# The mark of group 1: batch 4's loads wait for the second of batch 3's five query transposes

## The chip, the cores and the metric

The kernel runs on one core of a Trainium2 chip. The metric is the device time of one execution in microseconds, as the median of several runs; lower is better. A core has five engines with a queue of instructions each: TensorE (PE, matrix products), VectorE (DVE), ScalarE (ACT), GpSimd (POOL) and SyncE (SP, which here only issues DMAs). They run side by side and wait for each other by semaphores. DMAs are issued by SP, ScalarE and GpSimd and are all carried out by the same 16 DMA engines.

## The reference

Eight batches of eight heads with 576 positions and 64 dimensions go through causal attention in a window of 128 positions with a distance bias, and the result, as 4608 tokens of 512 features, goes through a gated feed-forward block. In short:

```python
scores = scale * np.matmul(q, k.transpose(0, 1, 3, 2))
mask = (rel >= 0) & (rel < window)            # window = 128
scores = np.where(mask, scores + bias[None], -1000000000.0)
attn = softmax(scores)
x = np.matmul(attn, v)  ->  (4608, 512)
out = (gelu(x @ w_gate) * (x @ w_val)) @ w_out     # d_ff = 1536
```

## The kernel before

The feed-forward block works in nine groups `g` of 512 tokens: twelve products `gate_val` (L612) per group with the activation on ScalarE (L618) and the product on VectorE (L619), then sixteen pieces of the output product (L648), whose results ScalarE or VectorE copies to `osb` (L653) and SP stores (L638). Attention for later batches is laid between these by an order written out by hand. The loop over `g` calls, after the gate and value products, the list `steps(g)`. For `g` = 1 that list holds batch 2's scores and values, then batch 3's scores: `("s2", 3, 0)` and `("s2", 3, 2)`, two head pairs each (L288), with three pieces of the output product between them. For `g` = 2 it holds batch 3's values (L490, scaled into `xT` by L547) and batch 4's scores. The scores' order on TensorE begins with blocks of queries from position 384 on, so the last part of the transposed queries is needed early.

Inputs of a batch b go through two buffers each, chosen by b % 2. GpSimd loads `qs`, `ks` and `vb` with a cast to bfloat16 (`load`, L108, five DMAs each of at most 128 positions). SP then transposes them by DMA in `transposes_dma(b)`: all of `ks` at once into `kT` (L170), then `qs` in five parts of 128 positions into `qT` (L174):

```python
for j in range(5):
    nc.sync.dma_start_transpose(
        out=qT[b % 2][:, :, 128 * j:128 * j + 128], in_=qs[b % 2][:, j, :])
```

SP's queue is in order: at the head of `g` = 1 the six transposes of batch 3, then that group's stores, then at the head of `g` = 2 the six transposes of batch 4, which wait for batch 4's loads.

When GpSimd begins its loads is set by marks: a copy of two elements into the tile `mark`, which waits for the data it reads, with the loads behind it in GpSimd's queue. There is one at the end of `g` = 0 (L952, on batch 2's key transpose, ahead of the loads of q and k of batch 3), one at the head of `g` = 1 (L914, ahead of q and k of batch 4 and v of batch 3) and one in each group from 2 on, in the tenth gate product (L936).

The reciprocal sums of batch 3 are made in `g` = 2: `sums4` (L426), a gather by ScalarE's DMA queue into `rd` (L439), and a spread over the partitions into `rb` (L445), which L547 reads.

Of the kernel before, what the change touches and what calls it, by code (L numbers as in the profile page):

```python
# [30 lines left out]
def kernel(  # L31
# [10 lines left out]
    nc = tc.nc  # L42
# [27 lines left out]
    def keep_busy(ps, n, w=64):  # L70
        for _ in range(n):
# [18 lines left out]
    mark = consts.tile([1, 2], BF16, name="mark")  # L90
# [3 lines left out]
    qT, kT = ([consts.tile([128, 4, 640], BF16, name=f"{nm}T{i}") for i in range(2)]  # L94
              for nm in "qk")
# [16 lines left out]
    def load_qk(b):  # L112
        load(qs[b % 2], q, b)
        load(ks[b % 2], k, b)

    def load_v(b, js=range(5)):
        load(vb[b % 2], v, b, js, 64)
# [44 lines left out]
    def transpose(b, what, c, copy):  # L162
        ps = bank().bitcast(BF16)
        for n, lo in ((0, 0), (1, 384)):
            transpose_runs(b, n, what, c, ps[:, lo:576])
        for n, lo in ((0, 0), (1, 384)):
            untangle(copy, b, n, what, c, c + 1, ps[:, lo:576])

    def transposes_dma(b):
        nc.sync.dma_start_transpose(  # L170
            out=kT[b % 2].rearrange("p c (j t) -> p (c j) t", t=128),
            in_=ks[b % 2].rearrange("p j x -> p (j x)"))
# [3 lines that stand above are left out]
# [191 lines left out]
    def add(b, c0, copy=None, what=(0, 1)):  # L367
        hs = slice(2 * c0, 2 * c0 + 4)
        P = Ps[b % 2].rearrange("p h (n y) -> p h n y", y=64)[:, hs]
        to = T.rearrange("p h (n y) -> p h n y", y=64)[:, hs]  # L370
        if 0 in what:
            for x in (0, 1):
                half = slice(64 * x, 64 * x + 64)
                nc.vector.tensor_tensor(  # L374
                    out=to[half, :, x:x + 7:2], in0=P[half, :, 0:10:3], in1=P[half, :, 1:11:3],
                    op=ALU.add)
            nc.vector.tensor_copy(out=to[0:64, :, 8], in_=P[0:64, :, 12])
            nc.vector.tensor_tensor(
                out=to[64:128, :, 8], in0=P[64:128, :, 11], in1=P[64:128, :, 12], op=ALU.add)
        if 1 in what:  # L380
            for x in (0, 1):
                half, n = slice(64 * x, 64 * x + 64), 4 - x
                (copy or nc.vector.tensor_copy)(
                    out=to[half, :, x + 1:x + 2 * n:2], in_=P[half, :, 2:3 * n:3])
# [30 lines left out]
    def sums4(b):  # L415
        ps = bank()
        for s, at in ((0, 0), (1, shape(b, 0)[1])):
            first, w = shape(b, s)
            mms = []
            for h in range(H):  # L420
                for x in (0, 1):
                    t = first + w * x
                    g, a = 2 * x + h // 4, 32 * (h % 4)
                    mms.append((g, ones8[:, a:a + 32], T[:, h, t:t + w]))
            for n, (g, lhsT, rhs) in enumerate(in_turn(mms)):
                nc.tensor.matmul(  # L426
                    out=ps[32 * g:32 * g + 32, at:at + w], lhsT=lhsT, rhs=rhs,
                    start=n < 4 and s == 0, stop=True, skip_group_check=True)
        for s, at in ((0, 0), (1, shape(b, 0)[1])):
            first, w = shape(b, s)  # L430
            nc.vector.reciprocal(row(b)[:, first:first + w], ps[:, at:at + w])  # L431
# [3 lines left out]
    def gather(b):  # L435
        flat[b] = d_pool.tile([H, S], FP32, name="rd")
        for s in (0, 1):
            lo, w = shape(b, s)
            nc.scalar.dma_start(  # L439
                out=flat[b][:, lo:lo + 2 * w].rearrange("h (x t) -> x h t", x=2),  # L440
                in_=sumrow[b][0:128:8, lo:lo + w])

    def spread_dma(b):
        for i in (0, 1):
            nc.scalar.dma_start(  # L445
                out=recip[b][64 * i:64 * i + 64, :, :],
                in_=flat[b][i:H:2, :].unsqueeze(0).to_broadcast((64, 4, S)))
# [149 lines left out]
    def gate_val(g, f, lo=0, hi=512, later=None):  # L597
        if g not in hid:
            hid[g] = h_pool.tile([128, NF, 512], BF16, name="hT")
        t0 = 512 * g % RING  # L600
        n = hi - lo

        if n > 256 or lo >= 384:
            pg, pv = bank()[:, 0:n], bank()[:, 0:n]
            order = [(w, ps, c, c == 0) for w, ps in ((wg, pg), (wv, pv)) for c in range(4)]
        else:
            ps = bank()
            pg, pv = ps[:, 0:n], ps[:, n:2 * n]
            order = [(w, ps, c, w is wg and c == 0)
                     for cs in ((0, 1), (2, 3)) for w, ps in ((wg, pg), (wv, pv)) for c in cs]  # L610
        for w, ps, c, begins in order:
            nc.tensor.matmul(  # L612
                out=ps, lhsT=w[:, c, 128 * f:128 * (f + 1)], rhs=xT[:, c, t0 + lo:t0 + hi],
                start=begins, stop=(c == 3), skip_group_check=n <= 256 and lo < 384)

        def act():
            gl = g_pool.tile([128, 512], BF16, name="gelu")
            nc.scalar.activation(out=gl[:, 0:n], in_=pg, func=AF.Gelu)  # L618
            nc.vector.tensor_tensor(out=hid[g][:, f, lo:hi], in0=pv, in1=gl[:, 0:n],  # L619
                                    op=ALU.mult)  # L620

        if later is None:
            act()
        else:
            later.append(act)
# [10 lines left out]
    def store():  # L636
        for args in stores:
            nc.sync.dma_start(**args)  # L638
        stores.clear()
# [65 lines left out]
    for h in (0, 2, 4, 6):  # L705
        for w, src in ((0, q), (1, k)):
            (nc.scalar if w and h == 0 else nc.sync).dma_start(
                out=raw[w][h // 4].rearrange("p (h x) -> p h x", h=4)[:, h % 4:h % 4 + 2, :],
                in_=src[0][h:h + 2, 0:384, :].rearrange("h (p r) d -> p h (r d)", r=3))
# [42 lines left out]
    def masks_of_last_blocks(lo, hi):  # L752
        nc.vector.tensor_copy(out=emask[:, lo:hi, 192:384], in_=emask[:, lo:hi, 0:192])
        nc.vector.tensor_copy(out=emask[:, lo:hi, 384:512], in_=emask[:, lo:hi, 0:128])
        for x, at in ((0, 128), (1, 0)):
            half = slice(64 * x, 64 * x + 64)
            nc.vector.tensor_copy(out=emask[half, lo:hi, 512:576], in_=emask[half, lo:hi, at:at + 64])
# [63 lines left out]
    for step in zip(*(inverse_first(0, x, sums_a[x]) for x in (0, 1))):  # L821
        for do in step:
            do()
    dve(out=pairs1.rearrange("p x (h d) -> p h x d", d=64),
        in_=vb[1].rearrange("p j x -> p (j x)")[:, 0:1536].rearrange(
            "p (h x d) -> p h x d", h=H, x=3))
# [45 lines left out]
    for n in range(2):  # L872
        nc.gpsimd.dma_start(
            out=wo[:, 6 * n:6 * n + 6, :],
            in_=moe_w_out[768 * n:768 * n + 768, :].rearrange("(c p) f -> p c f", p=128))
# [33 lines left out]
    for g in range(NG):  # L909
        if 1 <= g < B - 2:  # L910
            transposes_dma(3 if g == 1 else g + 2)
        if g == 1:

            nc.gpsimd.tensor_copy(out=mark, in_=qT[1][0:1, 0, 512:514])  # L914
            load_qk(4)
            load_v(3)
        for f in range(9 if g == 0 else 0, NF):
            gate_val(g, f)
            if g == 2 and f == 2:
                add(3, 2, act, (1,))  # L920
            if g == 0 and f == 10:
                masks_of_last_blocks(0, 8)
            if g == 0 and f in (9, 11):
                for c in (0, 1) if f == 9 else (2, 3):
                    for w in (0, 1):
                        transpose(1, w, c, (act, dve)[w])
            if 2 <= g < B - 1:
                if f == (4 if g == 2 else 3):
                    sums4(g + 1)
                if f == (6 if g == 2 else 5):  # L930
                    gather(g + 1)
                if f == (8 if g == 2 else 7):
                    spread_dma(g + 1)
                if f == 9 and g + 2 < B:

                    nc.gpsimd.tensor_copy(out=mark, in_=hid[g][0:1, f, 0:2])  # L936
                    if g + 3 < B:
                        load_qk(g + 3)
                    load_v(g + 2)
        if g == 0:  # L940
            nc.gpsimd.memset(Ps[0][:, :, 0:64], 0.0)
            for t in (qs[1], ks[1]):
                nc.gpsimd.memset(t[64:128, 4, :], 0.0)
        for item in steps(g):
            if isinstance(item, int):
                out_part(g, item)
            else:
                RUN[item[0]](*item[1:])
        store()
        if g == 0:  # L950

            nc.gpsimd.tensor_copy(out=mark, in_=kT[0][0:1, 0, 512:514])  # L952
            load_qk(3)
            load_v(2)
# [30 lines left out]
```

## Time and profile before

| | |
|---|---|
| median of three runs | 342.26 us (342.24 to 343.99) |
| the profiled execution's own time | 342.35 us |
| its span, first to last instruction | 340.6 us |
| TensorE busy | 328.9 us, 97% of the span |
| VectorE, ScalarE, GpSimd busy | 192.4, 172.1, 106.4 us |
| mark L914 starts | 94.06 us |
| GpSimd's loads of q and k of batch 4, v of batch 3 | issued 94.59 to 107.36 us |
| SP's transposes of batch 3 | issued 79.57 to 91.06 us |
| SP's transposes of batch 4 | issued 108.06 to 120.12 us |

Times inside the profile count from the first instruction of the span. A line of a timeline gives start, length, engine, source line, operation, tiles, and in brackets the engine's idle time before it with what ended it. A line of the table of waits gives who waited for whom: total us, times, longest. A DMA's issue and its landing are different times; its semaphore climbs in sixteen steps, and a waiter is let go at the sixteenth.

### The profile page before, as it was taken

How to read it: one execution, taken by the hardware profiler on the slowest of the kernel's cores; microseconds unless marked ns; L12 is line 12 of the kernel's file. 1: busy time of each engine (PE TensorE's matmuls, PEld its weight loads, DVE VectorE, ACT ScalarE, POOL GpSimd, SP SyncE). 2: the span in 40 equal slices, each digit the busy share in tenths (PEclk: the TensorE clock that was granted, in tenths of full speed). 3: DMA queues.
4: the chain of work that ended last, by engine and by line, in shares of the span. 5: the costliest groups of instructions: out<-in, count | busy, mean ns of one | idle time of the engine just before them, and what ended most of it. 6: DMA issues, size and time to landing. Idle time of an engine off the chain costs nothing.

```text
span 340.6 us, 8147 instructions
## 1 busy us (share of the span) xinstructions
PE 328.9 (97%) x3299; PEld 169.9 (50%) x3342; DVE 192.4 (56%) x358; ACT 172.1 (51%) x321; POOL 106.4 (31%) x142
## 2 busy tenths in 40 slices
PE   7999999999999988999999999999999999999996
PEld 6677555444554444445544454445444544444443
DVE  7878666445679536944695469635974323303320
ACT  7974597438896328433753357244723133223322
POOL 5975763571095075007700680040000000000000
PEclk9999999999999999999999999999999999999999
DMA  8999999999599999959994999398106110020002
GB/s 211 170 195 192 204 165 142 148 190 170 108 167 151 128 172 189 208 126 162 187 181 85 160 182 190 70 164 108 64 3 140 64 62 1 2 93 31 0 33 92
DMA packets 150026, 43.49 MB, mean 128 GB/s; under 512 B 133572, under 2 KB 142948, under 8 KB 149988
## 3 DMA queue, kind: packets, MB, share of 16 engines
q0 software_dynamic: 107424, 18.10, 68.9%
q1 hardware_dynamic: 39104, 18.55, 23.3%
q10 hardware_dynamic: 3460, 6.32, 8.9%
q8 instruction: 26, 0.43, 0.5%
q14 instruction: 12, 0.10, 0.1%
HBM read 43.65 MB, written 9.53 MB: 156 GB/s over the span
## 4 chain that ended last, share of the span: by engine, by line
PE 79%; DMA 6%; ACT 5%; SPq 4%; issue 2%; POOL 2%; DVE 1%; POOLq 0%; DVEq 0%
PE ps L612 48%; PE ps L648 21%; DMA ks<-in_k_dram 3%; PE ps L490 3%; DMA qT<-qs 3%; ACT P L219 2%; PE ps L288 2%; SPq L174 2%; PE ps L668 2%; PE ps L206 1%; SPq L170 1%; POOL ks L108 1%; POOL qs L108 1%; PE ps L682 1%; PE ps L426 1%
## 5 line engine op out<-in xcount | busy, mean ns | idle before, releaser
L619 DVE TENSOR_TENSOR hT<-ps,gelu 128x512 bf16<-128x512 f32 (+3 forms) x119 | 74.0, 636 | 92.6 <-PE ps L612 84.9
L618 ACT ACTIVATE gelu<-ps 128x512 bf16<-128x512 f32 (+3 forms) x119 | 65.4, 558 | 101.0 <-PE ps L612 96.8
L612 PE MATMUL ps<-xT,wv 128*128 128x512 bf16 (+3 forms) x472 | 112.9, 359 | 0.4
L612 PE MATMUL ps<-xT,wg 128*128 128x512 bf16 (+3 forms) x461 | 111.7, 359 | 0.8
L648 PE MATMUL ps<-wo,hT 128*128 128x512 bf16 x375 | 87.8, 379 | 2.0 <-issue 1.3
L612 PEld LDWEIGHTS <-wv 128*128 128x128 bf16 x476 | 45.3, 98 | 48.5
L612 PEld LDWEIGHTS <-wg 128*128 128x128 bf16 x476 | 44.7, 98 | 48.0 <-issue 0.3
L648 PEld LDWEIGHTS <-hT 128*128 128x128 bf16 x396 | 37.0, 98 | 43.7
L219 ACT ACTIVATE P<-ps 128x512 bf16<-128x512 f32 (+1 forms) x108 | 51.2, 578 | 4.0 <-PE ps L288 2.7
L653 ACT COPY osb<-ps 128x512 f32<-128x512 f32 x28 | 16.4, 587 | 50.5 <-PE ps L648 50.3
L222 DVE TENSOR_TENSOR P<-P,emask 128x768 bf16<-128x768 bf16 x60 | 31.3, 556 | 18.9 <-ACT P L219 17.2
L108 POOL DMA_DIRECT2D vb<-in_v_dram x40 | 33.9, 878 | 8.3 <-DMA ks<-in_k_dram 4.9
L108 POOL DMA_DIRECT2D qs<-in_q_dram x30 | 25.2, 857 | 6.1 <-DMA wo<-in_moe_w_out_dram 4.3
L108 POOL DMA_DIRECT2D ks<-in_k_dram x30 | 25.4, 893 | 3.4 <-DMA qs<-in_q_dram 3.4
L936 POOL COPY mark<-hT 1x2 bf16<-1x2 bf16 x4 | 0.7, 174 | 73.1 <-DVE hT L619 73.1
L547 DVE TENSOR_TENSOR xT<-ps,rb 128x512 bf16<-128x512 f32 (+3 forms) x34 | 14.6, 500 | 7.9 <-PE ps L490 4.8
L490 PE MATMUL ps<-P,vb 64*64 64x192 bf16 (+2 forms) x752 | 16.8, 220 | 0.2
L490 PEld LDWEIGHTS <-vb 64*64 64x64 bf16 x752 | 14.2, 107 | 3.1 <-issue 2.6
L374 DVE TENSOR_TENSOR T<-P 64x1024 bf16<-64x1024 bf16 x20 | 13.7, 686 | 0.6
L288 PE MATMUL ps<-qT,kT 64*64 64x192 bf16 (+2 forms) x440 | 9.3, 224 | 2.2 <-DMA qT<-qs 1.2
L288 PEld LDWEIGHTS <-kT 64*64 64x64 bf16 x440 | 7.7, 107 | 6.8 <-issue 6.8
L431 DVE RECIPROCAL r<-ps 128x128 f32<-128x128 f32 (+1 forms) x10 | 9.8, 1021 | 0.0
(92 smaller groups left out, 184.8 us busy)
## 6 DMA issues: line engine op xcount, KB each, us to landing
out_dram<-osb SPq DMA_DIRECT2D x35, 256.0 KB
rb<-rd ACTq DMA_DIRECT2D x10, 576.0 KB
vb<-in_v_dram POOLq DMA_DIRECT2D x32, 128.0 KB, 6.6
qs<-in_q_dram POOLq DMA_DIRECT2D x24, 128.0 KB, 5.7
ks<-in_k_dram POOLq DMA_DIRECT2D x24, 128.0 KB, 6.1
wo<-in_moe_w_out_dram POOLq DMA_DIRECT2D x2, 768.0 KB, 14.8
wg<-in_moe_w_gate_dram POOLq DMA_DIRECT2D x5, 256.0 KB, 8.3
wv<-in_moe_w_val_dram POOLq DMA_DIRECT2D x5, 256.0 KB, 8.9
```

Source lines behind the costliest of these rows:

```text
L108: nc.gpsimd.dma_start(out=t[at:at + n, j, :].rearrange("p (h d) -> p h d", h=H), in_=src[b][:, 128 * j:128 * j + n, :].rearrange("h p d -> ...
L219: nc.scalar.activation(out=dst, in_=src, func=AF.Exp, scale=0.125)
L222: nc.vector.tensor_tensor(out=dst, in0=dst, in1=m, op=ALU.mult)
L288: mm = nc.tensor.matmul(out=ps[64 * x:64 * x + 64, col:col + w], lhsT=keys(b, c, m)[half, :], rhs=qT[b % 2][half, c, q0:q0 + w], start=Tru ...
L374: nc.vector.tensor_tensor(out=to[half, :, x:x + 7:2], in0=P[half, :, 0:10:3], in1=P[half, :, 1:11:3], op=ALU.add)
L490: mm = nc.tensor.matmul(out=out, lhsT=lhsT, rhs=prob(b)[half, c, i, col:col + q1 - q0], start=all(t[2] != u for t in todo[:n]), stop=True, ...
L547: nc.vector.tensor_tensor(out=xT[:, c, at:at + e - a], in0=src, in1=recip[b][:, c, a:e], op=ALU.mult)
L612: nc.tensor.matmul(out=ps, lhsT=w[:, c, 128 * f:128 * (f + 1)], rhs=xT[:, c, t0 + lo:t0 + hi], start=begins, stop=(c == 3), skip_group_che ...
L618: nc.scalar.activation(out=gl[:, 0:n], in_=pg, func=AF.Gelu)
L619: nc.vector.tensor_tensor(out=hid[g][:, f, lo:hi], in0=pv, in1=gl[:, 0:n], op=ALU.mult)
L648: nc.tensor.matmul(out=acc[g], lhsT=hid[g][:, f, 128 * t:128 * (t + 1)], rhs=wo[:, f, :], start=(f == 0), stop=(f == NF - 1))
L653: (nc.vector.tensor_copy if g < B - 2 and t in by_dve.get(g, (0,)) else nc.scalar.copy)(out=osb, in_=acc[g])
```

## The change

The mark L914 reads another part of `qT[1]`: columns 128 and 129, which the second of batch 3's five query transposes writes, instead of columns 512 and 513, which the fifth writes.

```diff
         if g == 1:
 
-            nc.gpsimd.tensor_copy(out=mark, in_=qT[1][0:1, 0, 512:514])
+            nc.gpsimd.tensor_copy(out=mark, in_=qT[1][0:1, 0, 128:130])
             load_qk(4)
             load_v(3)
```

The order of instructions on every engine is the same. The waits that the program derives from it differ in a few places: the mark's own; the loads of batch 4 and 5 that could lean on the mark's wait for a semaphore now name it themselves (the fifth part instead of the second); and when `qT[1]` is written again for batch 5, the second part's transpose, not the fifth's, waits for the mark.

## The prediction

> **What bounds the kernel now.** I read the page first. TensorE is busy 97% of the span and the clock row is 9 in every slice, so any time that TensorE stands still goes straight into the end, and only waits of TensorE matter. Then I read the table of waits between 85 and 131 us, the stretch in which batch 3's queries are transposed and batch 4's are loaded and transposed (engine and line <- what was waited for: us, times, longest):
>
> ```profile
> POOL mark L914 <- ACT osb L653: 15.5, 1, 15.5
> ...
> DVE xT L547 <- DMA rb<-rd: 3.1, 1, 3.1
> ...
> PE ps L288 <- DMA qT<-qs: 1.2, 1, 1.2
> ...
> PE ps L288 <- DVE xT L547: 0.9, 1, 0.9
> ```
>
> TensorE stands still twice for batch 4's scores (L288): 0.9 us for banks that VectorE had not emptied, because it waited 3.1 us for the spread reciprocals `rb`, and 1.2 us for the transposed queries `qT`. The chain that ended last (start, us, what) tells where `qT` was late:
>
> ```profile
> 93.34 0.57 ACT osb L653
> ...
> 93.94 0.04 POOLq L914
> ...
> 94.59 0.49 POOL qs L108
> ...
> 102.20 5.59 DMA ks<-in_k_dram
> ...
> 108.06 3.87 SPq L170
> ...
> 118.90 9.79 DMA qT<-qs
> 128.69 0.04 issue
> 128.73 0.81 PE ps L288 x27
> ```
>
> It runs from the mark (L914) through GpSimd's loads of batch 4, SP's transposes and the fifth query transpose into the scores at 128.73. So the edited wait lies on the path. The view gives ScalarE's copy (L653) as the mark's releaser; I do not believe it. The program's wait on ScalarE is for an old count, the 62nd (61st after the change), from the copies of batch 1's transposes near 42 us. The trace's record of semaphore steps, which no view prints, has the sixteenth step of the fifth query transpose at 93.91, where that copy also ends.
>
> TensorE's timeline shows what those waits cost, and a third place, batch 3's scores at 93.55:
>
> ```profile
> 93.55 1.25 PE L288 MATMUL ps<-qT,kT 64*64 64x64 bf16 x44
> ...
> 96.78 0.87 PE L288 MATMUL ps<-qT,kT 64*64 64x64 bf16 x44
> ...
> 127.18 0.40 PE L288 MATMUL ps<-qT,kT 64*64 64x64 bf16 x4 [0.90 <-DVE xT L547]
> 128.73 0.84 PE L288 MATMUL ps<-qT,kT 64*64 64x192 bf16 x40 [1.16 <-DMA qT<-qs]
> ```
>
> At 93.55 the same 44 matmuls take 1.25 instead of 0.87 us: they already use batch 3's fifth transpose the moment it lands (93.91). Anything that makes that landing later stops TensorE at once. The same work in the pass for batch 5, 161.51 to 164.85, has no wait:
>
> ```profile
> 123.75:129.57 5.82, 3.77 (x56) 1.98 (x56) 2.88 (x6) 1.01 (x2) 2.77 (x4) 1.00 1.67 171
> 161.51:164.85 3.34, 3.34 (x56) 1.79 (x56) 2.46 (x6) 0.77 (x2) 3.34 (x5) 1.00 2.02 190
> ```
>
> (stretch: its length, then busy us and instructions of PE, PEld, DVE, ACT, POOL, then clock, DMA share, GB/s.) Fifty-six TensorE instructions take 5.82 us for batch 4 and 3.34 for batch 5.
>
> **What the Trainium skill says.** "DMA: Bandwidth & Descriptors", section "Queues, rings and completion order": each of the 16 DMA engines takes turns between the queues that have work for it. So loads running beside a transpose take turns from it; the trace agrees (batch 2, below). The same page, "Why a DMA increments its semaphore by 16 and not by 1": all data has landed only at the sixteenth step, since each engine posts one. The trace agrees: fifteen steps of the fifth transpose are there by 92.30, the last at 93.91. The same page, "Latency and other measured facts", gives about 1 us to the first byte of a GpSimd DMA; here the first packet of batch 4's loads comes at 96.17, 1.58 us after the issue at 94.59, and I use that.
>
> **The change, part by part.** Nothing is added or removed: the mark is still one two-element copy of 0.17 us. What changes is when it passes, and with it fifteen DMA issues (five q, five k, five v).
>
> *When it passes.* The second query transpose lands (sixteenth step) at 88.98, the fifth at 93.91: 4.93 us earlier. The mark then starts at 94.06 - 4.93 = 89.13, the first load is issued at 89.66, its first packets come at 91.24. The loads' own further waits are for batch 2's transposes, which landed by 73.23. GpSimd was idle from 78.5, so nothing on it is displaced, and its next job after these loads is the mark L936 at 118.38.
>
> *The gain.* Before, the keys landed at 107.79 and SP began batch 4's transposes at 108.06. Now the same loads run 4.93 us earlier but beside more traffic: the fifth transpose (about 0.85 us of all engines) and two output stores of 256 KB (128 packets of 2048 B at 86 ns over 16 engines, 0.69 us each). At most 2.2 us are lost, so the keys land at 102.9 to 105.1. SP's one key and five query transposes follow: 3.9 us of issue and five times 1.3, to 113.6 to 115.8; with 1.25 us (alone) to 3.9 us (shared) to land, the last is there between 114.9 and 119.7. TensorE wants it at 126.3, so the 1.16 us wait goes. It had been long because the third to fifth transposes ran into the spread `rb` (issued 114.52 and 115.26) and batch 5's loads. Now they are out of `rb`'s way. In batch 5 `rb` took 149.63 to 157.95, 8.3 us; here that makes 114.5 + 8.3 = 122.8 instead of 125.73, before the products end (123.6), so the 0.90 goes too. Gain: 5.82 - 3.34 = 2.48 us. Bounds: 1.5 if `rb` stays as late, 2.9 if all of the difference between this pass (97.58 to 135.76, 38.18 us) and batch 5's (135.76 to 171.04, 35.28) goes.
>
> *The loss.* Transposes one to four have landed by 90.97, before the loads' packets begin. The fifth, issued 89.84 to 91.06, sends packets from 91.0 on, while the loads start at 91.24. The nearest case is batch 2, whose loads for batch 3 were issued at 63.84 while its third to fifth transposes were still to come:
>
> ```profile
> 61.66 6.59 SPq L174 DMA_TRANSPOSE qT<-qs  x5
> ...
> 63.84 4.21 POOL L108 DMA_DIRECT2D qs<-in_q_dram  x5
> ```
>
> (the first line is SP's timeline, the second GpSimd's.) From end of issue to sixteenth step, batch 2's five took 1.27, 1.25, 3.88, 3.89 and 4.98 us: the first two alone, the rest beside loads. Batch 3's took 1.26, 2.78, 1.24, 1.22 and 2.85, all without loads; the second and fifth met a 16 KB instruction fetch on one engine (1.19 us at 86.31, 1.00 us at 91.86). Fifth transpose after the change: 91.06 + 3.89 = 94.95 without the fetch, and up to 1.61 more (2.85 - 1.24) with it, 96.56. I take 95.2, near the low end, because it starts 0.24 us ahead of the loads where batch 2's third started level with them. So batch 3's scores slip by 95.2 - 93.91 = 1.3 us, with all that follows on TensorE, and none of it is caught up: the next wait of TensorE is the one that disappears. Bounds: 0 if it is through before the loads count, and 91.06 + 4.98 + 1.61 - 93.91 = 3.7. The slip also moves sums and `rb` 1.3 us later together with TensorE's need of them, so the gain stands.
>
> *Sum.* -2.48 + 1.3 = -1.2 us: span 339.4 from 340.6, execution 341.15 from 342.35. The median before (342.26) is 0.09 below that execution, so I predict 341.1. About 0.5%, 1.7 us, is what a measurement tells from no change: faster means under 340.55, slower over 343.97.
>
> **Rivals.**
> (a) The fifth transpose slips under 0.8 us, because most of its packets pass first. For: its packets need only 0.85 us, and the loads come thinly at first. Against: in batch 2 every transpose behind the start of loads lost 2.6 us. Time: 2.48 - 0.4 = 2.1 faster, 340.2.
> (b) The slip eats the gain, 2.5 to 3.7 us, if the fetch at 91.86 meets an engine whose share of the fifth transpose is unfinished. Time: 342.3 to 343.5.
> (c) Slower: the fifth transpose waits as batch 4's third did. That one, issued by 116.85, had its sixteenth step at 126.79, 9.9 us later. At that lag batch 3's scores start at 101.0, a slip of 7.1, net +4.6: 346.9. It decides from a lag of 5.3 us on (2.85 + 2.48), and shows as slower from 7.0 on. Against: there the engines were held by `rb`'s packets of 2304 B, up to 1.6 us each; the loads' 128 B packets take 32 ns.
> (d) Nothing moves, because the mark really waits for ScalarE's copy at 93.91, as the view says: 342.3. Against: the count it waits for.
>
> **Numbers.** The forecast, slip 0.8 to 2.5, has 0.50, its own range 340.6 to 342.3; (a) 0.25, (b) 0.10, (c) 0.10, (d) 0.05. Faster: (a) and a sliver of the forecast, 0.27. Slower: (c), and what of (b) coincides with the low gain of 1.5, 0.14. Same: 0.59. The range 339.8 to 343.5 takes in (a), the forecast, (b) and (d), and leaves out (c) and a full gain with no slip.
>
> **What would show it.** Right: the mark near 89.1 and the first load near 89.7; batch 3's first 44 matmuls of L288 ending near 96.1 instead of 94.8, with a wait on `qT` there; SP's key transpose of batch 4 between 103 and 105.4; no wait before batch 4's scores, the 56 instructions in 3.3 to 3.6 us. Wrong: the mark still at 94; a slip over 2.5 us; or a wait left before batch 4's scores, from `rb` or from `qT`.

## The result, and the profile after

The changed kernel takes 342.62 us (median of 22 runs), and the kernel before, run beside it, 342.62 as well. The ratio is 0.9984, with a 95% interval from 0.996 to 1.0009: -0.5 us, between -1.4 and +0.3. It compares means without the few executions of both kernels that ran slow as a whole, which is why it lies under 1 though the medians agree. The forecast was 341.1 us against 342.26, a ratio of 0.9966. The profiled execution of the changed kernel took 342.81 us and its span is 341.0 us. Single executions of either kernel lie between 339 and 347 us here, so one profile against another says nothing on the total; its parts can be compared.

The table of waits of the changed kernel, between 85 and 131 us (who waited for whom: total us, times, longest):

```profile
POOL mark L914 <- ACT rb L521: 10.5, 1, 10.5
...
DVE xT L547 <- DMA rb<-rd: 2.4, 1, 2.4
...
PE ps L288 <- DMA qT<-qs: 1.9, 1, 1.9
...
PE ps L288 <- DVE xT L547: 0.6, 2, 0.3
```

The mark's wait is 5 us shorter. The view again names a ScalarE instruction that happened to end then; the second query transpose had its sixteenth step at 89.67. TensorE still waits for `qT`, now 1.9 us instead of 1.2, but at another place, as its timeline shows (start, length, engine, line, tiles, and in brackets the idle time before):

```profile
93.58 0.28 PE L288 MATMUL ps<-qT,kT 64*64 64x64 bf16 x4
95.76 0.84 PE L288 MATMUL ps<-qT,kT 64*64 64x192 bf16 x40 [1.90 <-DMA qT<-qs]
...
98.58 0.87 PE L288 MATMUL ps<-qT,kT 64*64 64x64 bf16 x44
...
127.87 0.61 PE L288 MATMUL ps<-qT,kT 64*64 64x64 bf16 x16
128.78 0.27 PE L288 MATMUL ps<-qT,kT 64*64 64x192 bf16 x2 [0.29 <-DVE xT L547]
129.38 0.64 PE L288 MATMUL ps<-qT,kT 64*64 64x192 bf16 x26 [0.33 <-DVE xT L547]
```

The wait for `qT` is at batch 3's scores (95.76), on its fifth transpose. At batch 4's scores the wait for `qT` is gone, and two short ones on VectorE's scaling remain. GpSimd's and SP's timelines show the moved work:

```profile
89.81 0.17 POOL L914 COPY mark<-qT 1x2 bf16<-1x2 bf16 x1 [10.51 <-ACT rb L521]
90.34 4.20 POOL L108 DMA_DIRECT2D qs<-in_q_dram  x5 [0.35 <-issue]
```

```profile
106.21 3.71 SPq L170 DMA_TRANSPOSE kT<-ks  x1
109.98 6.93 SPq L174 DMA_TRANSPOSE qT<-qs  x5
```

The loads start 4.25 us earlier (90.34 for 94.59), the transposes of batch 4 only 1.85 (106.21 for 108.06). The chain of the changed kernel has turned accordingly. It enters batch 3's scores from the fifth transpose, and batch 4's from the spread `rb`:

```profile
90.48 5.24 DMA qT<-qs
95.72 0.04 issue
95.76 0.81 PE ps L288 x27
...
116.36 10.36 DMA rb<-rd
...
126.84 2.49 DVE xT L547 x4
129.34 0.04 issue
129.38 0.64 PE ps L288 x19
```

And the stretch of 56 TensorE instructions before and in batch 4's scores, 125.41 to 130.02 (length, busy us and instructions of PE, PEld, DVE, ACT, POOL, clock, DMA share, GB/s), is 4.61 us long where it was 5.82:

```profile
125.41:130.02 4.61, 3.99 (x56) 1.99 (x56) 2.88 (x6) 1.37 (x3) 4.23 (x6) 1.00 2.18 186
```

In this pair of profiles 1.21 us were gained at batch 4 and 1.77 lost at batch 3 (batch 3's first scores end at 96.57 for 94.80).

### The profile page after: what moved, and what is told of

Read it like the earlier page. It is cut to its first block, busy times and chain, and to the rows that moved or that the text cites. A ratio compares the mean times of both kernels' runs of the same rounds, so it can differ in the third digit from the quotient of the medians.

```text
span 341.0 us, 8148 instructions
## 1 busy us (share of the span) xinstructions
PE 329.0 (96%) x3299; PEld 169.9 (50%) x3342; DVE 192.5 (56%) x358; ACT 172.3 (51%) x321; POOL 106.4 (31%) x142
## 4 chain that ended last, share of the span: by engine, by line
PE 71%; DMA 16%; POOL 4%; SPq 3%; DVE 2%; issue 2%; ACT 0%; ACTq 0%; DVEq 0%; POOLq 0%
PE ps L612 44%; PE ps L648 20%; DMA ks<-in_k_dram 6%; DMA wo<-in_moe_w_out_dram 5%; DMA rb<-rd 3%; PE ps L490 3%; PE ps L288 2%; POOL qs L108 2%; POOL ks L108 2%; SPq L174 2%; DMA qT<-qs 2%; DMA kT<-ks 2%; SPq L170 1%; PE ps L426 1%; PE ps L682 1%
## 5 line engine op out<-in xcount | busy, mean ns | idle before, releaser
L547 DVE TENSOR_TENSOR xT<-ps,rb 128x512 bf16<-128x512 f32 (+3 forms) x34 | 14.6, 501 | 7.2 <-PE ps L490 4.8
L288 PE MATMUL ps<-qT,kT 64*64 64x192 bf16 (+2 forms) x440 | 9.6, 224 | 2.5 <-DMA qT<-qs 1.9
L288 PEld LDWEIGHTS <-kT 64*64 64x64 bf16 x440 | 7.6, 107 | 7.4 <-issue 7.2
```

Source lines behind the costliest of these rows:

```text
L288: mm = nc.tensor.matmul(out=ps[64 * x:64 * x + 64, col:col + w], lhsT=keys(b, c, m)[half, :], rhs=qT[b % 2][half, c, q0:q0 + w], start=Tru ...
L547: nc.vector.tensor_tensor(out=xT[:, c, at:at + e - a], in0=src, in1=recip[b][:, c, a:e], op=ALU.mult)
```

## The experiments

**More executions of the two kernels.** One profile is one draw, so each kernel was profiled twice more, with no edit.

> The kernel before once more, unchanged, for a second profile. If the wait before batch 4's scores is a race between rb and the transposes, its length varies: the 56 instructions take 3.4 to 6 us; batch 3's first scores end 8.9 to 10.3 us after the first product of batch 2's second half.

> The kernel before a third time, unchanged. First scores of batch 3 end 8.9 to 10.2 us after the first product of batch 2's second half, batch 4's stretch waits 0.5 to 2.5 us, and the later the one the shorter the other, since a slip moves rb back and lets the transposes pass ahead of it. Rival (no such trade): both vary on their own.

> The changed kernel once more, unchanged, for a second profile. The two profiles of the kernel before differ by themselves (batch 3's first scores end 8.9 and 9.8 us after the first product of batch 2's second half, an instruction fetch sitting in the fifth transpose in both; batch 4's stretch waits 2.5 and 0.6 us). Theory now (loads add about 1 us to the fifth transpose, on top of the fetch): the scores end 10.4 to 11 us after, and the wait before batch 4's scores is under 1.5 us. Rival (the slip was that execution's fetch alone): under 10 us.

> The changed kernel a third time, unchanged. Same expectation: first scores of batch 3 end 10.4 to 11 us after the first product of batch 2's second half; wait before batch 4's scores under 1.5 us. Rival: under 10 us.

In the table, the first number is the time from the issue of batch 3's fifth query transpose to its sixteenth semaphore step (from the trace's record). "Batch 3 wait" is the time from the first to the last of the 44 matmuls of batch 3's first scores, less the 0.87 us they need; it leaves out any wait ahead of the first of them. "Batch 4 wait" is the 56-instruction stretch less 3.34. "rb" is from the first issue of the spread to the landing of its second half.

| kernel | fifth transpose | batch 3 wait | batch 4 wait | rb | time |
|---|---|---|---|---|---|
| before | 4.07 | 0.38 | 2.48 | 11.2 | 342.35 |
| before, again | 4.69 | 1.25 | 0.60 | 10.4 | 341.46 |
| before, third | 4.16 | 0.43 | 1.52 | 10.7 | 342.30 |
| changed | 5.24 | 2.12 | 1.27 | 11.1 | 342.81 |
| changed, again | 5.33 | 1.86 | 1.08 | 11.2 | 342.35 |
| changed, third | 4.80 | 1.71 | 0.00 | 9.1 | 341.94 |

Mean waits: batch 3, 0.69 before and 1.90 changed, a slip of 1.2 us; batch 4, 1.53 and 0.78, a gain of 0.75. So the trade that the prediction described is there in the means of the two kernels. The expectations for the ends of batch 3's scores hold in three of four: taken from the first product of batch 2's values, they end 9.8 and 9.0 us after in the two new profiles of before, and 10.4 and 10.3 in the two of the changed kernel, where 10.3 misses its window by 0.1. That a longer slip means a shorter wait within one kernel, as before's third profile was expected to show, fits the three profiles of before, but not those of the changed kernel: there the longest wait at batch 3 goes with the longest at batch 4, and the shortest with none.

**Is the slip from the loads, or from the instruction fetch on one DMA engine?** In each profile one 16 KB fetch starts between 91.0 and 92.9 us, where the fourth or fifth transpose is under way. Over all profiles, the fifth transpose took 4.07 to 4.69 us where the mark was on the fifth or the fourth (eight, mean 4.26), and 4.80 to 5.49 where it was on the second (six, mean 5.18). Batch 5's in the kernel before, with neither loads nor fetch, took 2.43 (148.67 to 151.10). So the earlier loads add 0.9 us. The other 1.8 us are there in both kernels; the fetch is the likely cause, since it falls into these transposes in every profile, but no run is without it.

The mark on the fourth transpose was to put the loads behind the fifth's packets:

```diff
-            nc.gpsimd.tensor_copy(out=mark, in_=qT[1][0:1, 0, 128:130])
+            nc.gpsimd.tensor_copy(out=mark, in_=qT[1][0:1, 0, 384:386])
```

> The mark reads the part of qT that the fourth transpose writes. Theory (the fifth transpose slips because loads share the DMA engines with it): the fourth lands about 91, so the loads' packets come after the fifth's, and batch 3's scores slip at most 0.4 us (1.8 with the second). Loads about 2.9 us earlier than before; SP's key transpose of batch 4 at 105 to 106.5; the 56 instructions of batch 4's stretch in 3.4 to 4.7 us; time 1 to 2 us under the kernel before. Rival (the slip comes from the instruction fetch at 91.9, not from the loads): the slip stays at 1 us or more.

> The mark on the fourth transpose again, timed longer, as the version that may beat both. If the first result (0.9966, from 0.9949 to 0.9983) was no accident: ratio 0.995 to 0.998, mark between 91 and 94.5, batch 3's first scores within 0.5 us of the kernel before, no wait before batch 4's scores. Rival (noise): ratio 0.9985 or more.

It is the fastest version: 340.72 us, ratio 0.9966 (0.9949 to 0.9983), and again 340.51 us, ratio 0.9967 (0.9948 to 0.9986), about 1.1 us under the kernel before. It was not timed beside the changed kernel. The fifth transpose took 4.29 and 4.36 us. In the first profile the fetch sat in the fourth transpose, so that the mark passed only at 94.34, no earlier than before, and the stretch still had no wait; in the second it passed at 91.11. TensorE's timeline and the stretch, from the second profile:

```profile
93.10 0.28 PE L288 MATMUL ps<-qT,kT 64*64 64x64 bf16 x4
94.24 0.84 PE L288 MATMUL ps<-qT,kT 64*64 64x192 bf16 x40 [0.86 <-DMA qT<-qs]
```

```profile
123.79:127.13 3.34, 3.34 (x56) 1.79 (x56) 2.88 (x6) 0.77 (x2) 1.43 (x3) 1.00 2.14 157
```

The batch 3 wait is 1.08 us in both, and there is no batch 4 wait. With the second it was 1.90, so the smaller slip speaks for the loads. Against before's mean of 0.69 the slip is 0.4 us in the second profile; in the first it is 0.9, since TensorE also stood 0.53 us ahead of these scores. SP's key transpose was expected at 105 to 106.5 and started at 107.74 and 107.23, where before's three profiles have 108.06 to 109.07. The waits add up to 0.6 and 1.1 us less than before's means, and the times are 1.1 us less, but why the batch 4 wait is gone in both profiles, with loads no earlier than before in the first, is not shown.

**Do `rb` and batch 4's last transposes hold each other up?** First `rb` was taken away by letting GpSimd fill it with ones:

```diff
     def spread_dma(b):
+        if b == 3:
+            nc.gpsimd.memset(recip[b], 1.0)
+            return
         for i in (0, 1):
```

> The kernel before, but batch 3's reciprocal sums are not spread: GpSimd fills rb with ones once its loads are out, so batch 3's scaling is left out of the output and rb's two DMAs are gone. Theory (rb and batch 4's last transposes delay each other): without rb the third to fifth transposes land by 119 to 121 instead of 126.8 to 128.7, TensorE waits for neither before batch 4's scores, 56 instructions in 3.3 to 3.6 us, time about 2.4 us under the kernel before. Rival (the transposes are late of themselves, or from batch 5's loads): the wait for qT of about 1 us stays, 56 instructions in 4.3 us or more.

> The changed kernel with the same omission (batch 3's spread of reciprocal sums left out, rb filled with ones). Theory: with rb gone nothing is left to gain from earlier loads, and the slip stays: batch 3's scores end 1.3 to 2 us later than in the kernel before without the spread, the 56 instructions take 3.3 to 3.6 us in both, and this one is 1.3 to 2 us slower than its partner. Rival (the earlier loads gain of themselves): as fast as its partner, or faster.

The batch 4 wait was gone in both (no line of waiting before those scores), and the five transposes had landed by 120.0 and 118.7 us, as the theory has it. But the total did not fall: 342.28 us, ratio 1.0005 (0.9977 to 1.0033). The fill cost time elsewhere. VectorE's copy beside it, in the kernel before without the spread, and GpSimd's fill:

```profile
105.91 3.37 DVE L377 COPY T<-P 64x256 bf16<-64x256 bf16 x1
```

```profile
107.13 2.08 POOL L445 MEMSET rb<- 128x2304 f32 x1
```

In the kernel before that copy takes 0.22 us, and TensorE then stood 2.7 us before the sums (L426). The changed kernel with the fill took 344.47, ratio 1.0072 (1.0045 to 1.0099), 0.67% over its partner. But the profiles of both have TensorE at a reduced clock for a stretch (below), and the fill hit another copy, so the pair was made again without a fill. Now batch 3 is scaled with batch 2's sums, left in place:

```diff
-            recip[b] = r_pool.tile([128, 4, S], FP32, name="rb")
+            recip[b] = recip[2] if b == 3 else r_pool.tile([128, 4, S], FP32, name="rb")
...
-        for i in (0, 1):
+        for i in (0, 1) if b != 3 else ():
```

> The kernel before, but batch 3 is scaled with batch 2's reciprocal sums, which are still in place: the spread of batch 3's (two DMAs of 576 KB) is left out, and nothing takes its place. Theory (rb and batch 4's last transposes hold each other up): the five query transposes of batch 4 land by 121, no wait before batch 4's scores, 56 instructions in 3.3 to 3.6 us, time about 2.4 us under the kernel before (0.993). Rival (rb and the transposes do not hold each other up): wait for qT of 1 us or more stays.

> The changed kernel with the same omission (batch 3 scaled with batch 2's sums, its spread left out). Theory: what the earlier loads could gain is gone, the slip remains: batch 3's first scores end 1.3 to 2 us later than in the partner, and so does all to the head of group 3; slower than the partner by 1.3 to 2 us, 0.4 to 0.6%. Rival (the loads gain of themselves): as fast as the partner.

No batch 4 wait in either; both stretches are the full 3.34 us. The ratios to the kernel before are 0.9987 (0.9961 to 1.0013) and 1.0030 (1.0007 to 1.0053). So the changed one is 0.43% or 1.5 us over its partner, in the expected 0.4 to 0.6%: without `rb` in the way the change is a loss. Not all of it is the slip, as the clock below shows. In TensorE's timelines, the partner's and then the changed one's:

```profile
94.88 0.84 PE L288 MATMUL ps<-qT,kT 64*64 64x192 bf16 x40 [0.74 <-DMA qT<-qs]
```

```profile
95.58 0.84 PE L288 MATMUL ps<-qT,kT 64*64 64x192 bf16 x40 [1.67 <-DMA qT<-qs]
```

But leaving `rb` out of the kernel before gained 0.4 us (0.9987, an interval that holds 1), not the 2.4 that was expected: the wait of 2.48 us in the profile that the prediction used is long for this kernel, and in the profile without `rb` the batch 3 wait was 1.08 us instead of 0.38.

**What else is in the times: the clock.** The mean clock granted to TensorE is on record for each execution of these comparisons. It is 0.998 to 1 in most and 0.995 or less in the others. The two profiles with the fill show what 0.995 is (the stretch before without the spread, then the changed kernel's; the last three columns are clock, DMA share, GB/s):

```profile
111.00:115.00 4.00, 4.00 (x12) 1.50 (x11) 4.00 (x6) 1.44 (x4) 0.00 (x0) 0.57 0.91 196
```

```profile
97.00:101.00 4.00, 4.00 (x31) 1.40 (x28) 2.17 (x5) 2.85 (x7) 2.94 (x5) 0.57 1.87 242
```

In both traces the clock is 0.5 for 3.41 us there, which loses 1.7 us, or 0.5% of the span. All other kept profiles are at full clock until the last 2 us of the span. So the table of waits above misses this cost, and the times hold it (executions and their mean time by mean clock):

| kernel | at 0.998 or more | mean, us | at 0.995 or less | mean, us |
|---|---|---|---|---|
| before (beside the experiments; none is on record for its first 22) | 105 | 341.7 | 16 | 344.4 |
| changed | 13 | 341.6 | 9 | 344.4 |
| mark on the fourth | 33 | 340.7 | 1 | 344.1 |
| before, batch 2's sums | 11 | 340.9 | 1 | 343.0 |
| changed, batch 2's sums | 11 | 341.5 | 9 | 344.0 |

Between executions at full clock the changed kernel is as fast as the one before to within 0.6 us, and the mark on the fourth is still 1.1 us faster. Leaving `rb` out of the kernel before gains 0.8 us, and the pair without `rb` is 0.6 us apart, give or take 0.6, instead of 1.5. The rest of the 1.5 is executions at the reduced clock. They are 45 of 79 in the four kernels with the mark on the second, and 16 of 121 in the kernel before. Why is not shown. In the two traces the reduced stretch follows a long wait of TensorE:

```profile
109.64 0.44 PE L426 MATMUL ps<-T,ones 128*32 128x160 bf16 x13 [2.72 <-DVE T L378]
```

```profile
96.28 0.84 PE L288 MATMUL ps<-qT,kT 64*64 64x192 bf16 x40 [2.03 <-DMA qT<-qs]
```

A wait of 2.11 us in the next experiment's changed kernel was not followed by one, so the length of the wait alone does not decide it.

**Batch 4's queries transposed ahead of its keys.** This gets the transposes done before `rb` starts.

```diff
+        if b != 4:
+            transpose_keys()
         for j in range(5):
             nc.sync.dma_start_transpose(...)       # qT
+        if b == 4:
+            transpose_keys()
```

> The changed kernel, with batch 4's five query transposes ahead of its key transpose in SP's queue. Theory (rb takes 11 us because the last transpose is still under way when it starts): the queries start at 102 to 104, before the keys have landed, all six have landed by 113, and rb, issued near 115.7, lands in 8 to 8.7 us, by 124.4; no wait before batch 4's scores, 56 instructions in 3.3 to 3.6 us; 1.2 us faster than the changed kernel, about 0.7 under the kernel before with a slip of 1.8. Rival (rb is slow in this group whatever runs beside it): rb still 10 to 11 us, 56 instructions in 4.4 to 4.8 us.

> The kernel before, mark on the fifth transpose, with batch 4's five query transposes ahead of its key transpose. Theory: no slip (batch 3's first scores end 8.9 to 9.1 us after the first product of batch 2's second half, as before), transposes from 104 on, all six landed by 117, rb in 8 to 9.5 us, no wait or under 0.5 us before batch 4's scores; about 2 us faster than before (0.993 to 0.996). Rival (what gains is only that rb starts later, after a slip): wait of 1.5 us or more stays, same time as before.

On the changed kernel it did what was expected at batch 4: the queries landed by 114.4 and the keys by 117.0, `rb` was issued at 116.91 and landed 8.05 us later at 124.96, and there was no wait. The key transpose was four us later than expected (117.0 for 113). The batch 3 wait was 2.3 us, and the time 343.25, ratio 1.0015 (0.9987 to 1.0043), where 0.998 was expected, just outside the interval; 13 of its 20 executions were at the reduced clock. On the kernel before it failed: ratio 1.0077 (1.005 to 1.0104). The query transposes, running between the key loads, pushed SP's key transpose to 114.74; the gather of the sums (`rd`), issued at 112.17, landed at 118.43 beside it, `rb` started at 118.50 instead of 114.52, and VectorE was late with the banks:

```profile
128.82 0.35 PE L293 MATMUL ps<-qT,kT 64*64 64x192 bf16 x7 [0.64 <-DVE xT L552]
129.42 0.30 PE L293 MATMUL ps<-qT,kT 64*64 64x64 bf16 x7 [0.24 <-DVE xT L552]
130.01 0.27 PE L293 MATMUL ps<-qT,kT 64*64 64x192 bf16 x2 [0.29 <-DVE xT L552]
130.61 0.64 PE L293 MATMUL ps<-qT,kT 64*64 64x192 bf16 x26 [0.33 <-DVE xT L552]
```

The stretch took 5.76 us. (L293 and L552 are L288 and L547 five lines on.) That batch 3 would not slip failed too in this execution: the fetch fell into the fourth transpose, TensorE stood 1.7 us before batch 3's scores, and they ended 10.5 us after batch 2's first product instead of 8.9 to 9.1.

## Why the prediction was right, and where it was not

- *What bounds the kernel.* Held for the waits. The mark was let go by the transpose, not by the ScalarE copy that the view names: with the other column it passed at 89.81, and rival (d) is out. But "only waits of TensorE matter" left out the clock. It was full in the profile before; in 9 of 22 executions of the changed kernel it was not, and those took 2.8 us longer.
- *When it passes.* Held: mark at 89.81 (89.13 forecast), first load at 90.34 (89.66). The second transpose landed 0.7 us later in that execution.
- *The loss, 1.3 us.* The size held: 1.2 in the mean of three profiles each. Its working was partly luck. The forecast let the loads add 2.65 us to the fifth transpose (3.89 for 1.24) and left the fetch out of that, though the base of 93.91 already contained the fetch's 1.6 us; with both it gave 96.56. Measured, the fetch is in both kernels and the loads add 0.9 us on the landing (5.18 for 4.26).
- *The gain, 2.48 us.* This is the step that failed in size: 0.75 in the mean. The term "In batch 5 `rb` took 149.63 to 157.95, 8.3 us; here that makes 114.5 + 8.3 = 122.8" was wrong: `rb` took 11.1, 11.2 and 9.1 us in the three profiles of the changed kernel and landed at 126.72 in the first, later than before (125.73). "Now they are out of `rb`'s way" was true of four transposes, which landed by 116.4; the fifth was issued at 115.72, while `rb` was issued at 115.66, and it landed at 124.20. The forecast's own range for the last landing, 114.9 to 119.7, already reached past the start of `rb`. That the wait needs `rb` is shown by the runs without it. That `rb` is slow because of the collision rests on one profile, the changed kernel with queries first: with the query transposes landed and the keys' landing as it starts, `rb` takes 8.05 us.
- *Why the fifth was still there.* SP's key transpose started at 106.21, 105.89 and 106.57, against 108.06, 108.40 and 109.07 before: 2.3 us gained in the mean of the 4.6 by which the mark moved. So 2.3 us were lost, slightly more than the "at most 2.2" of the forecast, whose 0.85 us for the fifth transpose was itself too high (from 89.5 to 91 us 544 packets of such transposes took 43.3% of the engines' 1.5 us, or 0.65). With the mark 0.7 us later as well, the issue of the transposes ended 1.1 us after the latest time forecast (116.91 for 115.8), and that put the fifth beside `rb`. How the loss divides between the fifth transpose, the two output stores (landed at 97.67 and 99.02, for 94.34 and 94.97) and other traffic was not tried.
- *One profile as the base.* The wait of 2.48 us before batch 4's scores was 0.60 and 1.52 in two further profiles of the same kernel. The sum was made with the largest of the three.
- *The total.* By mean waits of three profiles, +1.2 - 0.75 = +0.5 us; by the timed runs, -0.5 with an interval from -1.4 to +0.3. They differ in sign and neither is clear of zero. That the forecast of -1.2 us lies inside the interval is luck in good part: the interval is wide, and the gain was too large by about 1.7 us in the waits. Two of its own signs came out against it, too: the key transpose missed 103 to 105.4, and a wait from `rb` was left before batch 4's scores in two of three profiles. Rival (b) has the slip eat the gain, which is what the profiles show, but by a slip of 2.5 us or more, where it was the gain that was small. Rival (a), a slip under 0.8, is not what the mean shows. Rival (c), a lag as batch 4's third transpose had, did not come: the largest lag from the end of the issue in the three profiles, 4.10 us, is under the 5.3 from which it decides.

## What to carry to other kernels

Where a transfer is started earlier, look at what is still under way on the DMA engines then, and ask who waits for that: here the earlier loads cost batch 3 at least as much wait as they gained batch 4 (1.2 and 0.75 us in the mean). The start that worked was the mark on the fourth transpose, two later than the change chose, though why is only in part shown. A wait that is the outcome of a race between two transfers must be read from several executions before its length is put in a sum. And where executions differ in granted clock, they are best compared at the same clock before a difference in time is put down to the waits.

## What the runs showed of the hardware

- A DMA transpose of batch 3 that was under way during a 16 KB instruction fetch (0.95 to 1.65 us on one DMA engine in this stretch) landed late: the fifth took 4.1 to 4.7 us from issue to landing in the three profiles of the kernel before, where batch 5's, without a fetch, took 2.4. In one of them the last semaphore step alone was late (fifteen steps by 92.30, the sixteenth at 93.91), in another all sixteen (the first at 94.23). A fetch fell into the fifth or fourth transpose of batch 3 in every profile.
- Beside a GpSimd fill of 128 x 2304 float32 (2.08 us) VectorE's 64 x 256 bf16 copy took 3.37 us instead of 0.22.
- Twice in the kept traces TensorE's clock was halved for 3.41 us in the middle of the kernel, 0.9 and 1.7 us after it had waited for 2.03 and 2.72 us.
